# Moving silu's table load, a batch's landmark sums, w_in copies and GpSimd's load issues in a fused Nystrom attention and silu MLP kernel

## The chip, the cores and the metric

The kernel runs on one core of one Trainium2 chip. A core has five engines that each take their own list of instructions in order: TensorE (PE, matrix products; PEld is its loading of weights), VectorE (DVE), ScalarE (ACT), GpSimd (POOL) and SyncE (SP, which issues transfers). They wait for each other by semaphores. Data lie in SBUF; products arrive in PSUM, which the kernel divides into eight banks of 128 x 512 fp32. Transfers run on 16 DMA engines; most loads are issued from GpSimd's list, since they convert fp32 to bf16 on the way.

The metric is the device time of one execution in microseconds (us): 260.79 before, the median of three runs (260.73 to 262.19).

## The reference

For each of 8 batches and 8 heads, q, k and v are 576 x 64. Landmarks are means of 18 successive rows, 32 of them:

```python
q_lm = q.reshape(B, H, m, S // m, D).mean(axis=3)      # m = 32, S // m = 18
k_lm = k.reshape(B, H, m, S // m, D).mean(axis=3)
A  = sm(q, k_lm)       # softmax of scaled scores, 576 x 32
Bm = sm(q_lm, k_lm)    # 32 x 32
C  = sm(q_lm, k)       # 32 x 576
Z = Bm.transpose(0, 1, 3, 2) / (norm_1(Bm) * norm_inf(Bm) + 1e-06)
for _ in range(6):
    Z = 2 * Z - Z @ Bm @ Z
x = A @ Z @ C @ v      # heads side by side: 4608 tokens x 512
h = x @ w_in           # 512 x 2048
out = (h * sigmoid(h)) @ w_out
```

The norms are taken over each head's 32 x 32 matrix (norm_1 and norm_inf stand for numpy's matrix norms of order 1 and infinity).

## The kernel before

**The algebra.** The kernel never forms x. Per batch it makes the small matrix Z C v of each head (`zwT`, made by `z_mm` and `z_out`), multiplies it into w_in (`m_unit` or `m_pair`, result `mb`: 256 landmark rows x 2048), transposes the softmax A (`AT`), and computes h = A times mb directly: `l1_mm` (two matmuls of 128 x 128 by up to 320 columns for each of two groups of 128 hidden units, into PSUM tile `hps`), then silu on ScalarE (`l1_act`, L803, result `gT`), then the product with w_out in blocks of 128 tokens: `l2_mm` (16 matmuls of 512 columns a block into a bank `ops`, then a ScalarE copy to `ost`, L830, and a store from SyncE).

**The loop.** L936 runs over the batches b, and inside it 16 steps s (L951): steps 0 to 7 are the eight groups of hidden units for the first half of the tokens, 8 to 15 for the second. While batch b's MLP runs, the attention of batch b + 1 is worked out between its matmuls: scores and exponentials at the first steps (at s = d + 1 and d + 2, where d is 2 for b = 0 and 1 and 0 afterwards), the six iterations (`ns_mm`, `ns_step`) at the next, then `w_mm`, `x_out`, `z_mm`, and the product with w_in. The object `a` is the attention of batch b + 1, `a0` that of batch b. Batches 0 and 1 are `tiled` (products in 32 x 32 tiles, A in chunks of 128 tokens); from batch 2 on (`sub`) the scores of A are transposed by VectorE and shifted by GpSimd. The branch at L1007 (`s == d + 2 and a.sub`) runs in b = 1 to 6, once each; the branch at L1017 runs in b = 0.

**What sets the order.** The order is written out by hand: each engine takes its instructions in the order of the text, and `tc.manual_schedule()` (L77) leaves it so. `l2_mm(n)` emits the next n matmuls of a queue of blocks, and the counts `CNT` and `REST` (L841 to L844) say how many at each step, so the point at which a block of 16 ends, and its copy is emitted, follows from these counts. One `act` is ScalarE's silu; `table(func)` (L163) is a one-element activation on `spare` that makes the chip load func's table (rows L165: ACT_TABLE_LOAD, then ACTIVATE).

**PSUM.** Pools: `psh` two tiles of two banks (`hps`, scores of C `scp`, transposes `ctp` and `atp`, pairs `mpp`), `pso` two banks used in turn (`ops`, `wp`, `idle`, one half of `m_unit`'s `mp`), `psn` one bank (`bb` of the iterations, landmark sums `lmp`), `psa` one bank. A tile taken from a pool waits until all reads of the tile that held the buffer before are done.

**The head, before the loop.** q and k of batch 0 arrive, TensorE runs filler matmuls on zeros (`idle`), and the attention of batch 0 is worked out alone up to L931. The landmark sums of batch 1's first half of heads (`landmarks_pe`, 18 matmuls with the identity, L206) are put behind `z_mm` there: three ahead of the product with w_in, 15 behind the transposes of A; their ScalarE copies (`landmarks_out`, L213) come at L959.

**GpSimd.** Its list holds the issues of loads (`load_qk` L101, `load_v` L112, `load_w_in`, `load_w_out`), the multiplies of `a_norm` (L680: VectorE sum and reciprocal, then GpSimd's product `an`, L693), and, from batch 2 on, the landmark sums (`landmarks_pool`, L223: five additions, `lma` to `lmn`, for each half of the heads).

Of the kernel before, what the change touches and what calls it, by code (L numbers as in the profile page):

```python
# [9 lines left out]
BF = mybir.dt.bfloat16  # L10
# [33 lines left out]
def kernel(  # L44
# [9 lines left out]
    nc = tc.nc  # L54
# [28 lines left out]
    def ps2(nm):  # L83
        return psh.tile([128, 2, 512], FP, tag="h", name=nm)
# [832 lines left out]
    load_w_out(2)  # L917
    load_w_out(3)
    load_v(1)
    at = ps2("atp")  # L920
    a.z_mm(at[:, 1, :])
    a.z_out()
    lp = psn1("lmp")
    landmarks_pe(1, lp, 0, 2, (0, 3))

    def first_tokens():
        a.a_transpose(0, at[:, 0, :].bitcast(BF))
        a.a_out(nc.vector.tensor_copy)
        landmarks_pe(1, lp, 0, 2, (3, SEG))

    a.m_unit(0, nc.vector.tensor_copy, nc.scalar.copy, parts=2, between=first_tokens)  # L931

    ready = None
    for b in range(B):  # L936
# [14 lines left out]
        for s in range(NDC):  # L951
# [2 lines left out]
                a0.m_pair(a0.m_done)  # L954
            if s <= d and b == 0:
                l1(s)
                act(s)
                if s == 0:
                    landmarks_out(1, lp, 0, 2)  # L959
                    a0.m_unit(1, nc.scalar.copy, nc.scalar.copy)  # L960
                elif s == 1:
                    idle(lp[:, 256:512], 8, 256)
                elif s == 2:
                    landmarks_pe(1, lp, 2, 2)
                    landmarks_out(1, lp, 2, 2)
                transpose_qk(1, ORD[s])
# [5 lines left out]
            elif not nxt or s <= d:  # L972
                l1(s)
                act(s)
                n = cnt[s]
                if b == 1 and s == d:
                    a = Att(2)
                    a.lm_t(0, 2)
                if nxt and s == d and not a.early:
                    l2_mm(3)  # L980
                    n -= 3
                    a.a_pair()
                l2_mm(n)

            elif s == d + 1:
                l1(s)
                act(s)
                l2_mm(cnt[s])
                if b == 0:

                    transpose_qk(1, ORD[s])
                    a.lm_t(1)
                    a.bd_expand(0, 2, nc.gpsimd.tensor_copy)
                    for i in (1, 2):
                        a0.a_scores(i)
                        a0.a_max(i)
                a.b_scores()
                a.c_scores()
                a.b_max()
                a.c_max(0)  # L1000
                table(AF.Exp)
                if b == 0:
                    for i in (1, 2):
                        a0.a_shift(i)
                        a0.a_exp(i)
                a.b_exp()
            elif s == d + 2 and a.sub:  # L1007
                a.a_start()
                a.c_max(1)
                a.c_exp(0)  # L1010
                a.c_exp(1)
                a.a_exp_all()
                a.b_norm()
                l2_mm(cnt[s])
                table(AF.Silu)
                l1(s)
            elif s == d + 2:  # L1017
                n = cnt[s]
                a.a_start()
                a.a_scores(0)  # L1020
                a.a_scores(1)
                a.c_max(1)
                a.a_max(0)
                a.a_max(1)
                a.c_exp(0)
                a.c_exp(1)
                a.a_scores(2)
                a.a_max(2)
                for i in range(2):
                    a.a_shift(i)  # L1030
                    a.a_exp(i)
                a.b_norm()
                a.a_shift(2)
                a.a_exp(2)
                a.c_transpose(0)
                a.c_out(0)
                a0.m_unit(2, nc.vector.tensor_copy, nc.scalar.copy, pair=True)
                a.f_mm()
                a.b_scale()
                a.f_out()  # L1040
                l2_mm(n)
                table(AF.Silu)
                l1(s)
            elif b == 0:
                l1(s)
                r = s - d
                n = cnt[s]
                if r == 3:
                    nc.vector.tensor_tensor(out=parity, in0=mask[:, 0:2, 0],
                                            in1=mask[:, 2:4, 0], op=OP.add)  # L1050
                    a.ns_mm()
                    a.ns_step()
                    act(s - 1)
                    a0.m_unit(3, nc.vector.tensor_copy, nc.scalar.copy)
                    a0.a_norm(1)
                elif r == 4:
                    a.ns_mm()
                    a.c_transpose(1)
                    a.ns_step()
                    a0.a_norm(2)  # L1060
                    a.c_out(1)
                elif r == 5:
                    act(s)
                    a.ns_mm()
                    a.ns_step()
                    l2_mm(2)
                    n -= 2
                    load_v(2)
                    a.w_scale()
                    a0.a_transpose(1)  # L1070
                    a0.a_out(nc.scalar.copy)
                    a.a_norm(0)
                elif r == 6:
                    a.ns_mm()
                    a.ns_step()
                    act(s)
                    l2_mm(2)
                    n -= 2
                    a.ns_mm()
                    load_qk(3, (1, 0))  # L1080
                    a.a_norm(1)
                    a.ns_step()
                    load_qk(3, (3, 2))
                elif r == 7:
                    a.ns_mm(last=True)
                    act(s)
                    a.x_out()
                    l2_mm(2)
                    n -= 2
                    a.w_mm()  # L1090
                    a.w_out()
                    a.a_norm(2)
                    landmarks_pool(2, 0)
                elif r == 8:
                    a.z_mm(psa1("zt"))
                    a.z_out()
                    act(s)
                    l2_mm(n)
                    n = 0
                    landmarks_pool(2, 2)  # L1100
                    a.a_transpose(0)
                    a.a_out(nc.vector.tensor_copy)
                    transpose_qk(2, ORD[0])
                elif r == 10:
                    a.a_transpose(1)
                    a.a_out(nc.vector.tensor_copy)
                    transpose_qk(2, ORD[1])
                elif r > 11:
                    transpose_qk(2, ORD[r - 10])
                if s in h:  # L1110
                    act(s)
                if r in (9, 11):
                    a.m_pair(r - 9)
                l2_mm(n)
            elif s == d + 3:
                l1(s)
                act(s - 1)
                act(s)
                l2_mm(2)
                a.f_mm()  # L1120
                a.b_scale()
                a.f_out()
                a.w_scale()


                nc.gpsimd.tensor_copy(out=gate, in_=a.wsp[:, 0, :])  # L1126
                l2_mm(cnt[s] - 2)
                a.ns_mm()
            elif s <= d + 8:
                l1(s)  # L1130
                if s == d + 6:
                    a.w_mm()
                a.ns_step()
                act(s)
                if s == d + 4:
                    a.a_sum(0)
                elif s == d + 5:
                    a.a_sum(1)
                elif s == d + 6:
                    a.w_out()  # L1140
                    a.a_rec(0, 2)
                    a.a_mul(0)
                    a.a_mul(1)
                l2_mm(cnt[s])
                a.ns_mm(last=(s == d + 8))
            elif s == d + 9:
                l1(s)
                a.x_out()
                act(s)
                l2_mm(cnt[s])  # L1150
            elif s == d + 10:
                l1(s)
                a.z_mm()
                a.z_out()
                act(s)
                l2_mm(cnt[s])
            else:
                l1(s)
                act(s)
                if s in (d + 11, d + 13):  # L1160
                    a.m_pair(s - d - 11)
                n = cnt[s]
                if s == 15 and ready and ready.early:
                    l2_mm(3)
                    n -= 3
                    ready.a_pair()
                l2_mm(n)
# [62 lines left out]
```

## Time and profile before

| what | value |
|---|---|
| median of three runs | 260.79 us (260.73, 262.19, 260.79) |
| the profiled execution | 262.13 us, span 260.4 us from first to last instruction |
| busy: PE, DVE, ACT, POOL | 249.9 (96%), 166.2 (64%), 170.4 (65%), 132.8 (51%) us |
| mean granted TensorE clock | 0.991 |
| `ops` (w_out) matmuls | 592, 146.8 us busy |
| `hps` (mb) matmuls | 512, 82.9 us busy |
| silu `gT` | 128, 652 ns each |
| table loads | 16, 1283 ns each |
| `ost` copies 128 x 512 | 35 of them (and two of 128 x 256), 571 ns each |
| GpSimd's `lma` | 12, 2377 ns each |

The profile is of one execution. A line of it names the line of the program, the engine, the operation, out<-in tiles, and shapes as partitions x elements; in a timeline the first two figures are the start and the length in us from the start of the span, and a bracket at the end gives the idle time before the instruction and what ended it. Matmuls are pipelined, so the length of one (379 ns for 512 columns) is longer than the distance of two in a row (0.216 us). The granted clock is the share of TensorE's full clock; rows of 0.50 mean that its matmuls take twice as long.

### The profile page before, as it was taken

The page shows a single profiled execution, that of the slowest core. Times are in us where ns is not written, and L with a number is a line of the kernel's source. Part 1 is how long each engine was busy: PE and PEld are TensorE (multiplying, and loading weights), DVE is VectorE, ACT ScalarE, POOL GpSimd, SP SyncE. Part 2 cuts the span into 40 slices and gives each one's busy share as a digit, 9 for nine tenths or more (in the row PEclk, how much of TensorE's full clock was granted, in tenths as well). Part 3 has the DMA queues.
Part 4 walks back from the last instruction along what each step waited for, and adds up shares of the span by engine and source line. Part 5 has one row for each costly group of instructions (what it writes and reads, how often), then busy time and mean ns, then how long its engine had stood idle before and what let it go on. Part 6 is the DMA issues. An engine that isn't in the chain of part 4 may idle for free.

```text
span 260.4 us, 6656 instructions
## 1 busy us (share of the span) xinstructions
PE 249.9 (96%) x2768; PEld 139.0 (53%) x2768; DVE 166.2 (64%) x391; ACT 170.4 (65%) x311; POOL 132.8 (51%) x161
## 2 busy tenths in 40 slices
PE   8989999989899999999999999999999999999994
PEld 2646654454454556456645564545555564556553
DVE  5877876759895969777885788686977745000000
ACT  2276985677847685869575957597668857446511
POOL 7616518993699469845993298138923030100000
PEclk9997999999999999999999999999999999999998
DMA  7999999960529992895279617113621401121122
GB/s 220 195 209 207 207 208 208 224 149 5 141 24 219 228 210 49 115 192 137 55 132 205 110 45 132 42 35 111 107 66 40 120 25 42 41 80 43 42 81 82
DMA packets 30062, 31.16 MB, mean 120 GB/s; under 512 B 10960, under 2 KB 21456, under 8 KB 30032
## 3 DMA queue, kind: packets, MB, share of 16 engines
q0 software_dynamic: 14816, 17.76, 41.4%
q1 hardware_dynamic: 15216, 12.98, 16.7%
q8 instruction: 21, 0.34, 0.5%
q14 instruction: 9, 0.07, 0.1%
HBM read 36.70 MB, written 9.44 MB: 177 GB/s over the span
## 4 chain that ended last, share of the span: by engine, by line
PE 77%; ACT 6%; DVE 6%; POOL 5%; DMA 3%; issue 2%; ACTq 0%; POOLq 0%
PE ops L80 43%; PE hps L80 21%; DMA nat<-in_q_dram 3%; PE bb L80 3%; PE mp L80 2%; PE lmp L80 2%; POOL lma L229 2%; DVE cmx L448 2%; ACT L165 1%; PE sa L80 1%; ACT eC L458 1%; PE wp L80 1%; PE scp L80 1%; ACT ex L644 1%; PE mpp L80 1%
## 5 line engine op out<-in xcount | busy, mean ns | idle before, releaser
L80 PE MATMUL ops<-w_out_sb,gT 128*128 128x512 bf16 (+1 forms) x592 | 146.8, 374 | 0.0
L804 ACT ACTIVATE gT<-hps 128x576 bf16<-128x576 f32 (+2 forms) x128 | 82.6, 652 | 57.2 <-PE hps L80 56.4
L80 PE MATMUL hps<-AT,mb 128*128 128x288 bf16 (+2 forms) x512 | 82.9, 286 | 1.7 <-ACT gT L804 1.0
L80 PEld LDWEIGHTS <-gT 128*128 128x128 bf16 x592 | 53.8, 98 | 48.2 <-issue 9.0
L80 PEld LDWEIGHTS <-mb 128*128 128x128 bf16 x512 | 48.6, 98 | 28.6 <-issue 3.3
L203 DVE STREAM_TRANSPOSE qkT<-nat 128x576 f32<-128x576 f32 x32 | 39.3, 1244 | 0.3
L830 ACT COPY ost<-ops 128x512 f32<-128x512 f32 (+1 forms) x37 | 21.1, 571 | 14.3 <-PE ops L80 14.2
L229 POOL TENSOR_TENSOR lma<-nat 128x1152 f32<-128x1152 bf16 x12 | 28.5, 2377 | 0.0
L407 DVE SCALAR_TENSOR_TENSOR fx<-fx,bb 128x320 bf16<-128x320 bf16 (+1 forms) x39 | 17.0, 435 | 12.5 <-PE bb L80 12.3
L632 POOL TENSOR_TENSOR xs<-xs,nm 128x576 f32<-128x576 f32 x12 | 13.6, 1152 | 21.3 <-DVE nm L630 21.3
L770 DVE CAST mb<-mp 128x512 bf16<-128x512 f32 x28 | 18.0, 684 | 7.4 <-PE mp L80 7.4
L165 ACT ACT_TABLE_LOAD x16 | 20.5, 1283 | 1.1 <-PEq L1214 0.8
L688 POOL TENSOR_TENSOR an<-ex,arec 128x576 bf16<-128x576 bf16 x12 | 13.6, 1158 | 5.3 <-DVE arec L674 5.3
L1126 POOL COPY gate<-wsp 128x2 f32<-128x2 f32 x6 | 1.1, 184 | 28.6 <-DVE wsp L492 28.6
L80 PEld LDWEIGHTS <-fx 32*32 32x32 bf16 (+1 forms) x168 | 8.2, 93 | 12.3 <-DVE fx L407 4.4
L771 ACT CAST mb<-mpp 128x1024 bf16<-128x1024 f32 x14 | 14.2, 1012 | 0.1
L80 PE MATMUL bb<-fx 32*32 32x64 bf16 (+2 forms) x168 | 13.1, 205 | 0.6 <-DVE fx L407 0.3
L626 DVE STREAM_TRANSPOSE xs<-sa 128x576 f32<-128x576 f32 x12 | 8.7, 762 | 6.9 <-PE sa L80 6.9
L234 POOL TENSOR_TENSOR lmc<-lmb,lma 128x384 f32<-128x384 f32 x12 | 12.0, 998 | 0.9
L232 POOL TENSOR_TENSOR lmb<-lma 128x384 f32<-128x384 f32 x12 | 12.0, 996 | 0.9
L448 DVE TENSOR_REDUCE cmx<-scp 128x1 f32<-128x576 f32 x16 | 11.9, 751 | 0.5 <-PE scp L80 0.3
L659 DVE TENSOR_REDUCE arec<-ex 128x18 f32<-128x576 bf16 (+2 forms) x17 | 11.8, 694 | 0.0
(126 smaller groups left out, 263.8 us busy)
## 6 DMA issues: line engine op xcount, KB each, us to landing
out_dram<-ost SPq DMA_DIRECT2D x35, 256.0 KB, 2.0
v<-in_v_dram POOLq DMA_DIRECT2D x8, 576.0 KB, 6.8
nat<-in_k_dram POOLq DMA_DIRECT2D x15, 288.0 KB, 9.3
nat<-in_q_dram POOLq DMA_DIRECT2D x15, 288.0 KB, 10.1
w_in_sb<-in_moe_w_in_dram POOLq DMA_DIRECT2D x4, 512.0 KB, 15.2
w_out_sb<-in_moe_w_out_dram POOLq DMA_DIRECT2D x4, 512.0 KB, 14.1
raw<-in_k_dram SPq DMA_DIRECT2D x1, 576.0 KB, 4.1
raw<-in_q_dram SPq DMA_DIRECT2D x1, 576.0 KB, 5.0
```

The lines of the kernel that those rows point to most:

```text
L80: nc.tensor.matmul(out=o, lhsT=lhsT, rhs=rhs, start=start, stop=stop, skip_group_check=True)
L165: nc.scalar.activation(out=spare[:, 1:2], in_=spare[:, 0:1], func=func)
L203: nc.vector.transpose(out=o.rearrange("p (l t) -> p t l", t=SEG), in_=nat_t[b][:, j, :].bitcast(FP).rearrange("p (t l) -> p t l", l=L))
L229: nc.gpsimd.tensor_tensor(out=a1, in0=nat[:, :, 0:3 * w], in1=nat[:, :, 3 * w:6 * w], op=OP.add)
L407: nc.vector.scalar_tensor_tensor(out=n, in0=self.fx, scalar=2.0, in1=self.p, op0=OP.mult, op1=OP.add if self.tiled else OP.subtract)
L448: nc.vector.tensor_reduce(out=mx, in_=self.s[g][:, :, 0:HF], op=OP.max, axis=AX.XY, negate=True)
L632: nc.gpsimd.tensor_tensor(out=self.xs[:, i], in0=self.xs[:, i], in1=self.nm[:, i].unsqueeze(3).to_broadcast((128, 2, SEG // 2, L)), op=OP.add)
L688: nc.gpsimd.tensor_tensor(out=self.an[:, i].rearrange("p r t l -> p (r t) l"), in0=x, in1=r.unsqueeze(2).to_broadcast((128, SEG, L)), op=O ...
L770: nc.vector.tensor_copy(out=o[:, r, 0:512], in_=m[r])
L771: nc.scalar.copy(out=o[:, :, 512:1024], in_=m2)
L804: nc.scalar.activation(out=gT_t[b][:, 2 * s:2 * s + 2, o + c0:o + c1], in_=h[:, :, 0:c1 - c0], func=AF.Silu)
L830: nc.scalar.copy(out=ost[:, 0:hi - lo], in_=st["ps"][:, 0:hi - lo])
```

## The change

Six edits, all of them in the order of the text; no computation is added or taken away but three filler matmuls.

- The landmark sums of batch 1's first half of heads go to a bank of `pso` in place of `psn`; ten of the 18 matmuls stand ahead of `z_mm`, eight behind `z_out`, and their two copies on ScalarE follow at once. The tile `lmp` in `psn` is then taken at step 0 of the loop.
- The transposes of A and their copy come ahead of the product with w_in, whose `between` goes away.
- The second unit of the w_in product moves from step 0 to step 1, with its copies in halves and `act(1)` between them; five fillers stand at step 1 in place of eight.
- In the branch of batches 2 on (L1007), `table(AF.Silu)` stands directly behind the exponentials, ahead of `b_norm` and `l2_mm`, in place of behind `l2_mm`. In the branch of batch 1 (L1017) it stands behind the last `a_exp`, ahead of the third w_in unit and all that follows.
- That third unit comes ahead of `c_transpose(0)` and `c_out(0)`, and both of its copies are VectorE's.
- GpSimd's issues of v of batch 2 and q and k of batch 3 are spread over steps r = 3 to 6: v and the first ahead of `a0.a_norm(1)`, the others one at a time behind `a0.a_norm(2)`, `a.a_norm(0)` and `a.a_norm(1)`, where there were two pairs around `a.a_norm(1)`.

```diff
     load_v(1)
+    lp = pso1("lmp")
+    landmarks_pe(1, lp, 0, 2, (0, 10))
     at = ps2("atp")
     a.z_mm(at[:, 1, :])
     a.z_out()
-    lp = psn1("lmp")
-    landmarks_pe(1, lp, 0, 2, (0, 3))
-
-    def first_tokens():
-        a.a_transpose(0, at[:, 0, :].bitcast(BF))
-        a.a_out(nc.vector.tensor_copy)
-        landmarks_pe(1, lp, 0, 2, (3, SEG))
-
-    a.m_unit(0, nc.vector.tensor_copy, nc.scalar.copy, parts=2, between=first_tokens)
+    landmarks_pe(1, lp, 0, 2, (10, SEG))
+    landmarks_out(1, lp, 0, 2)
+    a.a_transpose(0, at[:, 0, :].bitcast(BF))
+    a.a_out(nc.vector.tensor_copy)
+    a.m_unit(0, nc.vector.tensor_copy, nc.scalar.copy, parts=2)
...
                 l1(s)
-                act(s)
                 if s == 0:
-                    landmarks_out(1, lp, 0, 2)
-                    a0.m_unit(1, nc.scalar.copy, nc.scalar.copy)
+                    act(s)
+                    lp = psn1("lmp")
                 elif s == 1:
-                    idle(lp[:, 256:512], 8, 256)
+                    a0.m_unit(1, nc.scalar.copy, nc.scalar.copy, parts=2,
+                              between=lambda: act(1))
+                    idle(lp[:, 256:512], 5, 256)
                 elif s == 2:
+                    act(s)
                     landmarks_pe(1, lp, 2, 2)
...
                 a.a_exp_all()
+
+                table(AF.Silu)
                 a.b_norm()
                 l2_mm(cnt[s])
-                table(AF.Silu)
                 l1(s)
...
                 a.a_exp(2)
+                table(AF.Silu)
+                a0.m_unit(2, nc.vector.tensor_copy, nc.vector.tensor_copy, pair=True)
                 a.c_transpose(0)
                 a.c_out(0)
-                a0.m_unit(2, nc.vector.tensor_copy, nc.scalar.copy, pair=True)
                 a.f_mm()
                 a.b_scale()
                 a.f_out()
                 l2_mm(n)
-                table(AF.Silu)
                 l1(s)
...
                     a0.m_unit(3, nc.vector.tensor_copy, nc.scalar.copy)
+                    load_v(2)
+                    load_qk(3, (1,))
                     a0.a_norm(1)
...
                     a0.a_norm(2)
+                    load_qk(3, (0,))
...
-                    load_v(2)
...
                     a.a_norm(0)
+                    load_qk(3, (3,))
...
-                    load_qk(3, (1, 0))
                     a.a_norm(1)
+                    load_qk(3, (2,))
                     a.ns_step()
-                    load_qk(3, (3, 2))
```

## The prediction

> **What bounds the kernel now.** I read the page's chain first, then the chain in order of time, then the granted clock by windows, and last the queues around each moved line.
>
> The page's shares of the chain that ended last:
>
> ```profile
> PE 77%; ACT 6%; DVE 6%; POOL 5%; DMA 3%; issue 2%; ACTq 0%; POOLq 0%
> ```
>
> TensorE carries it, so an edit counts only if it moves TensorE's queue or one of the few pieces that are not PE. The chain in order of time, from 45 us (start, length, what):
>
> ```profile
> 45.92 0.63 POOL an L693
> 46.56 2.33 POOL lma L229
> ...
> 57.70 0.32 DVE lmc L271
> 58.07 0.50 PE sa L80 x16
> ...
> 66.10 1.28 ACT L165
> 67.60 0.55 ACT gT L804
> 68.19 0.65 PE hps L80 x4
> ```
>
> From 43.8 to 68.2 the chain runs over GpSimd's landmark sums of batch 2, their scores and maxima on VectorE, the exponentials and silu's table; TensorE idles 0.84 us at 58.07 and 0.95 us at 68.19 and is continuously busy after that. So whatever happens before 46 us counts only as far as it moves the first `lma` (L229).
>
> Third, the clock windows (stretch, length, PE busy, ..., PEclk as the third figure from the end):
>
> ```profile
> 16.65:20.06 3.41, 2.69 (x95) 1.59 (x94) 2.09 (x10) 2.71 (x5) 0.97 (x2) 1.00 1.20 208
> 20.06:23.48 3.42, 3.17 (x31) 2.48 (x31) 2.31 (x6) 1.61 (x5) 3.42 (x6) 0.50 1.15 207
> ```
>
> The profiled execution (262.13 us: span 260.4 and 1.73 around it) had half a clock from 20.06 to 23.48 us, where the batch 1 landmark sums (15 matmuls, 1.81 us; 18 take 1.17 at full clock) held up the first `l1` until 23.28. At full clock these 15 take 15 x 0.057 = 0.86 from about 21.1 and end at 21.97, when the three ScalarE copies of w_in's product (1.07 from 20.95) are nearly done too: 1.31 earlier. The profiled time is 1.34 over the median of 260.79, so I take the median run to be one without that window.
>
> **The head, edits one by one.** The landmark sums: 18 before and after, ten now beside the wait for `x_out` (TensorE idle 19.33 to 19.76, ten take 10 x 0.057 = 0.57, so `z_mm` comes up to 0.1 later) and eight beside `z_out`; their two copies (0.34) go to ScalarE where it is free after its table (20.65). A^T (4 matmuls 0.61, copy 0.43) ahead of the w_in product (8 matmuls 0.41): 0.3 later for the product, but the first `l1` no longer waits for landmark sums: about 21.7. The second w_in unit split around `act(1)` and five idles for eight (1.03/8 = 0.13 each) let `l1(2)` start before all four copies are done: about 0.15. All this is at most 0.5 us against the median run, 1.3 against the profiled one. Around 33 us silu's table moves ahead of a w_in copy that now goes to VectorE: ScalarE's wait (0.45) and copy (0.59) leave its queue, VectorE gets 0.68 more ahead of `c_out` and `b_scale`, so `f_out` ends 0.7 later, 0.1 behind the point at which TensorE asks for it (35.95). Net 0 to 0.2 lost there.
>
> What does it bring at `lma`? Two clocks stand before it. One is GpSimd's queue: four `nat` issues (1.14 and 1.13 us) stood between `an` 42.6 and 45.92; two of them are moved, worth up to 1.1. The other is the load. A landing time (the last figure, us from issue) and a wait that shows how GpSimd's issues are paced:
>
> ```profile
> nat<-in_q_dram POOLq DMA_DIRECT2D x1, 288.0 KB, 15.2
> POOL nat L108 <- DMA w_out_sb<-in_moe_w_out_dram: 1.0, 1, 1.0
> ```
>
> The first is batch 2's q half, issued 29.86: lands 45.06, behind a queue that has moved 207 GB/s without a pause since 5 us. `lma` reads it, so it can't start before about 45.36 (0.3 is what the other wait shows from landing 31.66 to issue 31.94): 1.15 before the profiled 46.5, and no earlier whatever GpSimd does. The wait says that the 20th issue waited for the 12th to land (the 10th and 11th waited for the 2nd and 3rd). So in the new places batch 3's first half, the 22nd, waits for the third w_out load (21.78 + 15.0 = 36.8), ahead of `a0.a_norm(1)`: its multiply starts at about 37.6 (38.34 before; about 37.0 in the median run). The 24th waits for v (23.26 + 18.9 = 42.2), the 25th for batch 2's first half (29.31 + 14.3 = 43.6); `a_norm(2)` ends near 45.2. GpSimd is thus paced by landings, and `lma` comes at 45.36 with or without the slow clock. In the median run GpSimd's old order gives 42.4, 43.45, 44.8, 45.45: the same landing. So the head gains 1.15 against the profiled execution and 0 against the median (bounds: 0.4 gained, 0.6 lost if `a_transpose(1)`, now at 39.3 behind that multiply, costs more than TensorE's slack at 58.07). Take 0. GpSimd's issues with v and batch 3 cost no one else: same order, and their data is used after 68 us.
>
> **The table in the sub-batch branch.** This is the edit with a price. In L1007-1016, run once each in b = 1 to 6, the load moves from behind `l2_mm` to ahead of it. `l2_mm` emits, when a block of 16 matmuls is full, the copy `ost` (L830) that frees its PSUM bank; that copy is now queued on ScalarE behind the table load (1.28) and silu's first use (0.20). ScalarE in b = 3 now (start, length, what):
>
> ```profile
> 117.55 1.15 ACT L639 ACTIVATE ex<-xs 128x1152 bf16<-128x1152 f32 x1
> 118.60 0.57 ACT L830 COPY ost<-ops 128x512 f32<-128x512 f32 x1
> 119.19 1.28 ACT L165 ACT_TABLE_LOAD   x1
> 120.48 0.20 ACT L165 ACTIVATE spare<-spare 128x1 f32<-128x1 f32 x1
> 120.59 1.17 ACT L804 ACTIVATE gT<-hps 128x576 bf16<-128x576 f32 x2
> ```
>
> The copy follows the exponential without a gap, so the load gains nothing by passing it: silu still starts at 120.59. The copy ends at about 120.69 (exponential to 118.70, load to 120.00, first use, copy from 120.12), not 119.17. Who waits? The pool `pso` has two banks, so the first matmul of the block after next. TensorE in that stretch, and the `ops` matmuls started before 119.57:
>
> ```profile
> 118.94 2.32 PE L80 MATMUL ops<-w_out_sb,gT 128*128 128x512 bf16 x10
> L80 PE MATMUL ops<-w_out_sb,gT x192: 379/379/390, 34.1 to 119.4; 128*128 128x512 bf16 x192
> ```
>
> 192 is 12 x 16: the next block's first matmul is the fourth of those ten, 118.94 + 3 x 0.216 = 119.59. It needs the bank whose copy ends at 120.69; with 0.06 to wake (silu's end 177.54 to `hps` 177.60) it starts at 120.75: **1.16 us lost**. The same count for the others. b = 2: 128 matmuls started before 93.43, so the ninth block begins at 93.43; exponential to 91.90, copy to 93.89, wake 93.95: **0.52**. b = 5: 336 before 175.69; exponential to 175.02, copy to 177.01, start 177.07 against 175.70: 1.37, of which 0.20 was already lost (`hps` at 177.60 waits for silu, 0.39 behind the matmul before it instead of 0.19): **1.17**. b = 4 and 6 end their second block one matmul into the next step (149.79 against a copy to 148.49), and in b = 1 the block after next begins after 72 us: 0. Sum **2.85 us**, with nothing behind it to give it back: TensorE is busy 30.00 of 30 us from 100 to 160.
>
> Sum on the profiled execution: 262.13 - 1.15 + 2.85 = 263.83; on the median, 260.79 + 0 + 2.85 = 263.64. I say 263.7, 1.1% over the median; about 1% (2.6 us) is what a measurement of this kernel tells from no change.
>
> **What the Trainium skill says.** TensorE: Matmul & The Clock Gate, section "Why this matters for your kernels", has the clock drop only after gaps of about 3 us; by that rule my stalls of 0.5 to 1.2 us cost themselves alone and the sum stays. The row above speaks against it: the longest gap from 16.65 to 20.06 was 0.43 us, and the clock fell.
>
> **Rivals.**
> 1. The copies come in time (the other side). A bank is late only if the 1.5 us by which the copy moves exceed its margin now: 93.43 - 92.38 = 1.05, 119.59 - 119.17 = 0.42, 175.70 - 175.49 = 0.21. If the exponentials end 1.3 us earlier against TensorE, nothing is lost, and the head decides: 260.4 to 261.3, not slower. Against: the scores and maxima ahead of them are where they were. 0.07 (0.01 of it below 258.2).
> 2. Part is given back: `lma` sits on GpSimd's issues in the median run too, so the head gains up to 1.1, or later waits such as the 0.2 in b = 5 absorb it: 261.6 to 262.8. The landing of 45.06 speaks against. 0.13.
> 3. The head loses: `a0.a_norm(1)` behind a later landing, past the slack at 58.07: 264.4 to 265.2. 0.06.
> 4. A stall starves a clock window: 3.41 us at half clock lose 1.7 us each, 265.3 for one, 268.7 for three. The 0.95 us gap at 67.2 to 68.2 among dense matmuls left the clock at 1.00, which speaks against. 0.06.
> 5. A load behind a long exponential first empties the engine for as long as a load lasts: three stalls by 1.3 more, 267.5. 0.02.
> The Trainium skill, ScalarE: Activation LUTs, section "What ACT_TABLE_LOAD costs", states such a drain, 1.38 us beside a load of 1.28; by it the three stalls would be 7.0 us and the time 267.8. The rows differ: the ten loads after 86 us start 0.02 behind the instruction before them (114.00 behind a silu that ended at 113.98).
>
> The forecast holds 0.66, by itself 263.1 to 264.4 (`lma` between 0.6 and 1.3 earlier than profiled; the stall in b = 2 between 0 and its 0.5), 0.46 of it above the 263.4 that is 1%. Slower 0.46 + 0.06 + 0.06 + 0.02 = 0.60, within 0.39, faster 0.01. The range reaches over rival 2 and half of rival 3: 261.6 to 264.9.
>
> **What will show it.** ScalarE's list with the load directly behind `ex` and `ost` behind it in b = 2, 3, 5; `ops` waiting for `ost` there, about 0.5, 1.2, 1.4; the same places in b = 4 and 6 without a wait; `lma` at 45.2 to 45.6; the first `l1` near 22. Wrong if `ops` shows no wait for L830, or if `lma` starts well before 45.

## The result, and the profile after

The changed kernel takes 263.47 us (median of 8 runs, 262.97 to 263.54). The kernel before, run beside it, has a median of 261.53 (8 runs, 260.69 to 262.34). The ratio is 1.0071, with a 95% interval of 1.0048 to 1.0094: slower, by less than 1%.

To read this ratio one must know that executions of the kernel before come in two kinds. Some have a granted clock of 0.997 or more and take 260.4 to 261.2 us; the others have 0.991 to 0.993 and take 261.9 to 262.4, which is the window at half a clock that the prediction found in the profiled execution. Over all comparisons of this study 45 of 117 executions before were of the second kind (one more, a disturbed one of 266.4 us, is left out). The changed kernel had none in 8. So the change costs 2.8 us against the first kind, 1.2 against the second, and 0.7% against the mixture. Below, "full clock" and "half clock" name the two kinds; before they have medians of 260.71 and 262.29.

The profiled execution after is 263.16 us (span 261.4). Its shares of the chain that ended last:

```profile
PE 70%; ACT 9%; DVE 9%; POOL 5%; issue 3%; DMA 2%; ACTq 0%; POOLq 0%
```

ScalarE has 9% where it had 6. The 3% of issue are not to be read as time: this profile lists 554 `ops` matmuls in place of 592, and where a record is missing, the trace shows a short idle time without a cause. The other waits of TensorE (what waits, line, for whom; us in total, times, longest):

```profile
PE ops L80 <- issue: 4.1, 26, 0.2
PE ops L80 <- ACT ost L830: 2.5, 3, 1.2
PE idle L80 <- DVE zero L130: 1.3, 1, 1.3
PE hps L80 <- ACT gT L804: 1.0, 1, 1.0
```

The second line is new. Three times the w_out matmuls wait for `ost`, ScalarE's copy out of a PSUM bank. One of them in the timeline, b = 3 (start, length, what; in brackets the idle time before it and who ended it):

```profile
116.28 1.15 ACT L639 ACTIVATE ex<-xs 128x1152 bf16<-128x1152 f32 x1
...
117.44 1.28 ACT L165 ACT_TABLE_LOAD   x1
...
118.74 0.20 ACT L165 ACTIVATE spare<-spare 128x1 f32<-128x1 f32 x1
118.85 0.57 ACT L830 COPY ost<-ops 128x512 f32<-128x512 f32 x1
...
119.31 1.19 ACT L804 ACTIVATE gT<-hps 128x576 bf16<-128x576 f32 x2
...
119.47 1.67 PE L80 MATMUL ops<-w_out_sb,gT 128*128 128x512 bf16 x7 [0.99 <-ACT ost L830]
```

The load stands directly behind the exponential, the copy behind the load, and the seven matmuls start 0.05 behind the copy's end at 119.42. The three matmuls ahead of them started at 117.67, so without the wait the next would have come at 117.67 + 3 x 0.216 = 118.32: 1.15 us are lost. The other two places:

```profile
92.21 1.02 PE L80 MATMUL ops<-w_out_sb,gT 128*128 128x512 bf16 x4 [0.35 <-ACT ost L830]
...
176.92 1.46 PE L80 MATMUL ops<-w_out_sb,gT 128*128 128x512 bf16 x6 [1.20 <-ACT ost L830]
```

Worked out in the same way from the rows ahead of them, they lose 0.51 (92.21 against 90.40 + 6 x 0.216) and 1.36 (176.92 against 174.91 + 3 x 0.216). The brackets are smaller than the losses, since they count from the modelled end of the matmul before.

The first half of the chain, in order of time:

```profile
43.59 0.40 POOL nat L108
43.98 0.17 issue
44.16 0.63 POOL an L693
44.78 2.33 POOL lma L229
...
55.94 0.32 DVE lmc L271
56.30 0.50 PE sa L80 x14
...
62.80 1.05 ACT ex L639
63.87 1.28 ACT L165
65.19 0.09 issue
65.27 0.57 ACT ost L830
65.84 0.56 ACT gT L804
66.44 0.65 PE hps L80 x4
```

`lma` starts 1.77 us before its place in the profile of before (46.50), which is of the half-clock kind. In the kernel's old order at full clock it starts at 45.00 (traces of experiments 2 and 3), so against that it gains 0.27. In b = 1 the copy `ost` stands between table and silu, where it delays no bank. The clock (stretch, length, then for each engine busy time and instructions, PEclk third from the end):

```profile
16.84:20.25 3.41, 2.61 (x104) 2.02 (x98) 2.20 (x10) 2.96 (x5) 1.25 (x3) 1.00 1.20 209
20.25:23.67 3.42, 2.87 (x39) 1.70 (x37) 2.94 (x6) 2.55 (x10) 3.42 (x5) 1.00 1.18 208
```

Where the profile of before had 0.50 there is 1.00.

### The profile page after: what moved, and what is told of

Read it like the earlier page. It is cut to its first block, busy times and chain, and to the rows that moved or that the text cites. A ratio compares the mean times of both kernels' runs of the same rounds, so it can differ in the third digit from the quotient of the medians.

```text
span 261.4 us, 6609 instructions
## 1 busy us (share of the span) xinstructions
PE 242.5 (93%) x2723; PEld 137.0 (52%) x2765; DVE 166.2 (64%) x392; ACT 170.5 (65%) x312; POOL 133.1 (51%) x161
## 4 chain that ended last, share of the span: by engine, by line
PE 70%; ACT 9%; DVE 9%; POOL 5%; issue 3%; DMA 2%; ACTq 0%; POOLq 0%
PE ops L80 38%; PE hps L80 20%; PE bb L80 3%; DVE cmx L448 3%; ACT L165 2%; PE lmp L80 2%; PE mp L80 2%; POOL lma L229 2%; ACT ex L639 2%; DMA raw<-in_k_dram 2%; ACT eC L458 1%; PE sa L80 1%; POOL an L693 1%; PE wp L80 1%; ACT ost L830 1%
## 5 line engine op out<-in xcount | busy, mean ns | idle before, releaser
L80 PE MATMUL ops<-w_out_sb,gT 128*128 128x512 bf16 (+1 forms) x554 | 139.7, 373 | 7.0 <-issue 4.1
```

The source lines that it names most:

```text
L80: nc.tensor.matmul(out=o, lhsT=lhsT, rhs=rhs, start=start, stop=stop, skip_group_check=True)
```

## The experiments

For each kernel the medians at full and at half clock are given, with the number of runs, and the ratio with its interval to all runs of the kernel before on the same chip.

**1. The table edit taken back.** After, but for the branch of batches 2 on.

```diff
-                table(AF.Silu)
                 a.b_norm()
                 l2_mm(cnt[s])
+                table(AF.Silu)
```

> The changed kernel with one edit undone: in the branch of batches 2 on, silu's table stands behind l2_mm again. Theory S (the table edit in b = 2, 3 and 5 is the whole loss, 0.51 + 1.15 + 1.36 us in the changed kernel's trace): 263.47 - 2.8 = 260.6 to 260.8, with no wait of ops for ost, and all runs close together (260.4 to 261.0), since the changed kernel showed no execution with a half clock in the head. Theory H (the head's edits or GpSimd's issues carry a part of the loss): 261.5 or more in runs at full clock.

Measured: 260.72 in all 12 runs' median (260.53 to 261.02), none at half clock; 0.9983 [0.9965, 1.0002]. No `ops` matmul waits for a copy. The one edit is worth 263.47 - 260.72 = 2.75 us, and all others together 0.0 at full clock.

**2. The table edit alone**, the same two lines the other way round in the kernel before.

> The kernel before with that edit alone. Theory S: 2.7 us on top of either group of before's runs, so 263.4 at full clock (before 260.7) and 264.9 where the head has its half clock (before 262.2); waits of ops for ost of about 0.5, 1.15 and 1.35 us. Theory H: under 262.5 in the faster runs.

Measured: 263.44 (4 runs) and 265.05 (2 runs); 1.0106 [1.0073, 1.0140]. The waits of TensorE show the same line as after:

```profile
PE ops L80 <- ACT ost L830: 2.5, 3, 1.2
```

Its price is 2.73 at full clock and 2.76 at half clock: it adds to the window of the head and does not depend on it.

**3. The early table only where no bank should be late**, in b = 1, 4 and 6 of the kernel before.

```diff
                 a.a_exp_all()
+                if b in (1, 4, 6):
+                    table(AF.Silu)
                 a.b_norm()
                 l2_mm(cnt[s])
-                table(AF.Silu)
+                if b not in (1, 4, 6):
+                    table(AF.Silu)
```

> The kernel before with the table ahead of l2_mm only in b = 1, 4 and 6, where the block after next begins after its bank's copy. Theory S (a bank that comes late, not the order itself, is the price): no change, 260.7 and 262.2 by group, no wait of ops for ost. Rival O (each early load costs something of its own, by an order on ScalarE that is worse everywhere): half of the six moves, about 1.4 us slower.

Measured: 260.85 (8 runs) and 262.24 (4 runs); 1.0005 [0.9982, 1.0027]. The largest waits of TensorE, in which `ops` is absent:

```profile
PE idle L80 <- DVE zero L130: 1.3, 1, 1.3
PE lmp L80 <- DVE qkT L203: 1.2, 1, 1.2
PE hps L80 <- ACT gT L804: 1.0, 1, 1.0
```

The order itself costs nothing to be seen (0.1). The price sits in b = 2, 3 and 5, the steps that the count of blocks had named.

**4. The table stays early, the copies go to VectorE** (after, in that branch only), so that nothing is queued behind the load.

```diff
-    def l2_mm(n):
+    def l2_mm(n, copy=nc.scalar.copy):
...
-                nc.scalar.copy(out=ost[:, 0:hi - lo], in_=st["ps"][:, 0:hi - lo])
+                copy(out=ost[:, 0:hi - lo], in_=st["ps"][:, 0:hi - lo])
...
-                l2_mm(cnt[s])
+                l2_mm(cnt[s], nc.vector.tensor_copy)
```

> The changed kernel with the ost copies that fall into the step of the early table load given to VectorE. Theory S: TensorE waits for the copy, not for ScalarE as such, so the three waits of ops for ost vanish and the time is at most that of the kernel with the table put back, 260.7; moreover in b = 1 silu starts a copy (0.5 us) earlier and TensorE's wait for it there (1.0 us) shrinks by that: 260.2. Rival V (VectorE, which has scores, b_scale and the transposes to do at that time, hands the delay on): 261 or more.

Measured: 260.55 (12 runs, 260.11 to 261.02, none at half clock); 0.9963 [0.9943, 0.9983]. The copy in b = 1, and what is left of the wait for silu:

```profile
63.04 0.68 DVE L830 COPY ost<-ops 128x512 f32<-128x512 f32 x1
...
64.18 1.28 ACT L165 ACT_TABLE_LOAD   x1
```

```profile
PE hps L80 <- ACT gT L804: 0.5, 1, 0.5
```

The three waits are gone with the table still early, so it is the copy in ScalarE's queue and not the load that TensorE waited for. The wait for silu falls from 1.0 to 0.5, but the kernel is only 0.17 faster than with the table taken back. Where the other 0.3 goes was not found.

**5. The head's edits alone** (landmark sums, A^T, w_in's second unit) on the kernel before.

> The kernel before with the head's edits alone (landmark sums around z, A^T ahead of w_in, second w_in unit around act(1), five fillers). If the ten sums in the wait for x_out keep the clock up: no run with a half clock between 18 and 24 us, all runs 260.5 to 261.0. If the half clock has another cause (where the executions fall against the clock's windows): two groups about 1 us or more apart as before. First l1 at about 21.8 in a run at full clock, and the first lma (L229) no more than 0.4 us earlier than at full clock before, since a landing paces it.

Measured: 260.50 (12 runs, 260.17 to 260.67, none at half clock); 0.9972 [0.9954, 0.9991]. At full clock they gain 0.2. In the trace the first `l1` starts at 21.82 and `lma` at 44.75, 0.25 before its 45.00 in the old order. What they do beside that is to make the half clock go away. All kernels of this study that have these edits, the changed one among them, show no run at half clock in 92; four that have the old head (experiments 2, 3, 6 and 7) show 14 in 42.

**6. GpSimd's issues alone** on the kernel before.

> The kernel before with GpSimd's issues alone moved. Theory L (the first lma is paced by landings in either order: the 24th issue waits for v, the q half of batch 2 lands at 44.4 to 45.0): no change at full clock, 260.6 to 260.9, lma at 44.9 to 45.1; and with the half clock in the head less of a loss, since GpSimd's queue no longer carries it on: the slower group falls from 262.2 to about 261.2. Rival G (GpSimd's own issues set lma): up to 1.1 faster in both groups.

Measured: 260.82 (6 runs) and 261.73 (6 runs); 0.9996 [0.9975, 1.0018]. At full clock nothing, as expected. At half clock 0.56 less than before, about half of what was expected: the window costs 0.9 in place of 1.58. In its profiled execution (half clock) `lma` starts at 46.13, only 0.37 before its place in the profile of before. The new places are not enough to make GpSimd's late start good. The place that was expected at full clock, 44.9 to 45.1, is not tested: this is the only trace.

**7. The table and w_in copies around 33 us alone.**

```diff
                 a.a_exp(2)
+                table(AF.Silu)
+                a0.m_unit(2, nc.vector.tensor_copy, nc.vector.tensor_copy, pair=True)
                 a.c_transpose(0)
                 a.c_out(0)
-                a0.m_unit(2, nc.vector.tensor_copy, nc.scalar.copy, pair=True)
...
                 l2_mm(n)
-                table(AF.Silu)
```

> The kernel before with the edits of the branch of batch 1 alone (silu's table behind the last a_exp, third w_in unit ahead of c_transpose and copied by VectorE). By the prediction 0 to 0.2 us lost there and nothing at the end, since lma does not move: 260.7 to 260.9 at full clock, two groups as before.

Measured: 260.67 (10 runs) and 261.92 and 262.23 (2 runs); 0.9976 [0.9954, 0.9998]. No loss.

**8. Which part of the head keeps the clock: the ten sums in the gap?** After with the table taken back, and all 18 landmark sums behind `z_out`, none beside the wait for `x_out`.

```diff
     lp = pso1("lmp")
-    landmarks_pe(1, lp, 0, 2, (0, 10))
     at = ps2("atp")
     a.z_mm(at[:, 1, :])
     a.z_out()
-    landmarks_pe(1, lp, 0, 2, (10, SEG))
+    landmarks_pe(1, lp, 0, 2, (0, SEG))
```

> The changed kernel with the table put back and with all 18 landmark sums behind z_out, none in the wait for x_out. Theory C (the ten sums in that wait keep the clock up): executions with a half clock from about 20 us come back, as a part of the runs 0.3 us or more above the rest, less than the 1.4 of before because lma is paced by landings. Rival: the clock holds without them, and all runs stay within 260.5 to 261.1.

Measured: 260.78 (12 runs, 260.47 to 261.15, none at half clock); 0.9973 [0.9953, 0.9994]. The clock holds without the ten matmuls in the gap, so that theory falls.

**9. Or the bank?** The kernel before, with nothing changed but the pool of the landmark sums, which then need not wait until `z_out` has read the bank.

```diff
     a.z_out()
-    lp = psn1("lmp")
+    lp = pso1("lmp")
     landmarks_pe(1, lp, 0, 2, (0, 3))
...
                     landmarks_out(1, lp, 0, 2)
+                    lp = psn1("lmp")
```

> The kernel before with the landmark sums' bank alone changed (pso for psn), so that the three sums behind z_mm need not wait for z_out (0.3 us) and nothing else moves. If that idle stretch is what lets the clock fall: no slower group, all runs near 260.7. If it is the sum of the head's rearrangement (A^T, no 15 sums in front of the first l1): two groups as before, 260.7 and 262.2, about a third of the runs in the slower.

Measured: 260.57 (12 runs, 260.29 to 260.91, none at half clock, while 9 of 28 runs of the kernel before on that chip were); 0.9974 [0.9954, 0.9994]. The first three sums in the timeline of before, and of this kernel:

```profile
20.31 0.48 PE L80 MATMUL lmp<-nat,ident 128*128 128x128 bf16 x3 [0.31 <-DVE zwT L541]
```

```profile
19.78 0.34 PE L80 MATMUL lmp<-nat,ident 128*128 128x128 bf16 x3
```

The wait of 0.31 is gone, and no run is at half clock. At the share of the kernel before (45 of 117) none in 12 would come by chance once in some 300 times, at 9 of 28 once in 100, so the change of bank very probably removes it. How is not shown, and the wait itself can hardly be the cause: in the profile of before it lasts from 20.00 to 20.31, and the clock had fallen at 20.06.

**10. Head and early table with VectorE's copies**: experiments 4 and 5 together, with GpSimd's issues and the stretch around 33 us as before.

> The kernel before with the head's edits, silu's table ahead of l2_mm and the ost copies of that step on VectorE; GpSimd's issues and the branch of batch 1 as before. The head's edits alone gave 260.50; the copy on VectorE took TensorE's wait for silu in b = 1 from 1.0 to 0.5 us, so 260.2 (0.3 to 0.5 less) with no slower group. If VectorE hands delays on, 260.5 or more.

Measured: 260.37 (12 runs, 260.09 to 260.74, none at half clock); 0.9966 [0.9947, 0.9985]. Of the early table's 0.5 in b = 1 only 0.13 shows against experiment 5.

**11. Is `lma` held by GpSimd's issues or by the landing?** Experiment 10 with all four loads of batch 3 behind the landmark sums.

```diff
-                    load_qk(3, (1, 0))
                     a.a_norm(1)
                     a.ns_step()
-                    load_qk(3, (3, 2))
...
                     landmarks_pool(2, 2)
+                    load_qk(3)
```

> The same with the four loads of batch 3 issued behind the landmark sums of batch 2 instead of between the three a_norm. Theory L: GpSimd is then free for lma once the q half of batch 2 has landed (44.4 to 45.0 in the runs so far) and a_norm(2) is done (about 43.9), so lma comes at 44.4 to 44.8, at most 0.4 earlier: 259.9 to 260.2. Rival G (the issues were what held it): lma at 43.9 and 0.9 us gained.

Measured: 261.40 (12 runs, 260.83 to 262.01); 1.0010 [0.9990, 1.0030], 1.0 over experiment 10. With the issues out of the way `lma` waits for the load, 0.27 before its place in experiment 10:

```profile
44.37 2.37 POOL L229 TENSOR_TENSOR lma<-nat 128x1152 f32<-128x1152 bf16 x1 [0.23 <-DMA nat<-in_q_dram]
```

The gain is lost 15 us later. VectorE scales a column of maxima, `bbs`, in experiment 10 and here:

```profile
59.62 0.44 DVE L304 TENSOR_SCALAR bbs<-bmx 128x2 f32<-128x2 f32 x1
```

```profile
59.35 1.71 DVE L304 TENSOR_SCALAR bbs<-bmx 128x2 f32<-128x2 f32 x1
```

and TensorE then waits for the exponentials of C, 1.1 us at once:

```profile
PE hps L80 <- ACT eC L458: 1.5, 3, 1.1
```

**12. Only the second pair of issues moved**, to the step of b = 1 behind `a_pair`, past the stretch that experiment 11 disturbed.

```diff
                     a.a_norm(1)
                     a.ns_step()
-                    load_qk(3, (3, 2))
...
                     a.a_pair()
+                    if b == 1:
+                        load_qk(3, (3, 2))
```

> The kernel with the head's edits and the ost copies on VectorE, with only the second pair of batch 3's loads moved, to behind GpSimd's two additions of b = 1 (L632, ended at 61.1 us). Theory L: lma comes with the landing, 44.1 to 44.4, 0.3 earlier, and since GpSimd's two additions again wait for VectorE one by one, the scaling bbs (L304) takes 0.44 and not the 1.71 us that it took where all four loads had been put behind the landmark sums: 260.0 to 260.2. If that 1.71 came from the later loads themselves and not from how GpSimd's and VectorE's instructions met, it is there again: 261 or more.

Measured: 260.02 (12 runs, 259.56 to 260.33, none at half clock); 0.9946 [0.9926, 0.9967]. `bbs` takes 0.44 again, and `lma` again waits for the load:

```profile
45.10 2.37 POOL L229 TENSOR_TENSOR lma<-nat 128x1152 f32<-128x1152 bf16 x1 [0.81 <-DMA nat<-in_q_dram]
```

This is the fastest kernel of the study, 0.5% under the one before (0.7 us, or 0.3%, under its runs at full clock) and 1.3% under the changed one (3.45 us). But `lma` was expected at 44.1 to 44.4, and here it is later than in experiment 10 (44.64). The profiled execution is the kernel's slowest (260.33), with a late landing; in the others the load may land earlier, but no trace shows it, so where the 0.35 over experiment 10 comes from stays open.

## Why the prediction was right or wrong

**The table edit: right in place, cause and size.** The prediction had 0.52, 1.16 and 1.37 us for b = 2, 3 and 5 and nothing for 1, 4 and 6. The trace has 0.51, 1.15 and 1.36, in these three places only; experiment 3 shows the other three to be free, experiments 1 and 2 the edit to be the whole loss, experiment 4 the queued copy to be its cause. The sum was 2.85; the trace gives 3.02, less the 0.20 that b = 5 lost before, 2.82; the times give 2.75 and 2.73. What made it come out was to count blocks of 16 from the number of matmuls started, so that the matmul which needs the late bank was known by its place and its start. Rival 1 (the copies come in time) and rival 2 (part given back) are out.

**The other edits at full clock: right.** 0 was forecast with bounds of 0.4 gained and 0.6 lost; experiment 1 measures 0.0. The single pieces lie between 0.2 gained (head) and 0.1 lost (GpSimd), and around 33 us the loss of up to 0.2 did not come, so rival 3 is out. The first `l1` starts at 21.80 (21.7 forecast), only 0.07 before its place in the old order at full clock (21.87, experiments 2 and 3).

**The landing as the bound of `lma`: the mechanism right, the size off.** The rows of GpSimd in the profile after:

```profile
36.68 0.54 POOL L108 DMA_DIRECT2D nat<-in_k_dram  x1 [1.73 <-DVE fx L407]
37.29 1.62 POOL L693 TENSOR_TENSOR an<-ex,arec 128x512 bf16<-128x512 bf16 x2
...
41.87 0.59 POOL L108 DMA_DIRECT2D nat<-in_k_dram  x1 [1.06 <-DMA v<-in_v_dram]
...
44.73 2.37 POOL L229 TENSOR_TENSOR lma<-nat 128x1152 f32<-128x1152 bf16 x1
```

The 24th issue waits for v, as was worked out, and the multiply comes at 37.29 (37.6 forecast). But `lma` started at 44.73, outside the 45.2 to 45.6 that were forecast. Two terms of "no earlier than 45.36" were too large: the load lands at 44.4 after (issued 28.11, 16.3 us), not 45.06, and the 0.3 taken for the wake-up is 0.08 in experiment 12 (issued 28.12, 16.9 us, start 45.10) and 0.17 in experiment 11 (28.10, 16.1, 44.37). So at full clock landing and issues end nearly together: `lma` waits for neither alone in the changed kernel, and for the landing once the issues are moved (experiments 11 and 12).

The prediction put the old order at full clock at the same 45.36 and had no trace of it. Experiment 3 has one:

```profile
45.00 2.37 POOL L229 TENSOR_TENSOR lma<-nat 128x1152 f32<-128x1152 bf16 x1
```

Both places were thus forecast late by about as much (0.36 and 0.63), and their difference, which is what counts, came out at 0.27, and at 0.09 in experiment 1 (`lma` at 44.91), where 0 was forecast. The sum held because both places were off the same way. Rival 2 had up to 1.1 here, and no gain reached the end in experiment 1.

**The half clock: the window was read rightly, its place in the sum was not.** The step that failed is "I take the median run to be one without that window". The 260.79 shown was such a run, but more than a third of the executions are not, so the kernel before measures 261.53 beside the changed one. The absolute time was then close (263.7 said, 263.47 measured, within 263.1 to 264.4), while the difference was 1.9 instead of 2.85 and fell under 1%, where 0.60 had been put on more. The step also let GpSimd's pacing by landings make the slow clock indifferent. Experiment 6 shows that the new issues bring back 0.56 of 1.58. What takes the window away is the new head (0 of 92 runs) and very probably already its change of bank (experiment 9), which the prediction counted only for its place in the queue. That the changed kernel would have no run at half clock was nowhere argued; as far as its median rests on that, the close absolute time is luck.

**The stalls and the clock.** Rival 4 (a stall starves a window) did not come: stalls of 0.5 to 1.4 us left the clock at 0.997 or more in all 8 runs. With that the rule of the Trainium skill, TensorE: Matmul & The Clock Gate, section "Why this matters for your kernels", agrees, which asks for no gap over about 3 us if the clock is to stay up. The head speaks against it: in the profile of before the clock fell at 20.06 behind gaps of at most 0.43 us.

**The drain.** Rival 5 did not come either. The Trainium skill, ScalarE: Activation LUTs, section "What ACT_TABLE_LOAD costs", has 1.38 us of draining beside a load of 1.28; here the exponential ended at 117.43, the load started at 117.44 and took 1.28.

## What to carry to other kernels

Before a long instruction is moved forward in an engine's queue, list what is thereby queued behind it, and for each of these find the buffer it frees and the instruction that takes that buffer next: with two banks, the first matmul of the block after next, whose start can be counted out of the trace (here the three losses came out to within 0.01 us). If the queued work is a copy out of PSUM, give it to another engine before moving the load. And look at the spread of the times shown: three runs with one 1.4 us off may be two kinds of execution, and a change that removes one of them shifts the median without touching the other.

## What was not expected of the hardware

**Whether the half clock comes seems to hang on where the clock's windows begin, and on the order of the head.** The kernel before has it in 45 of 117 executions, 1.58 us each. In its profile the clock fell at 20.06 and once more behind the last matmuls, at 258.99; in that of experiment 6 at 20.54 and 259.47. Both pairs lie 238.93 us apart, which is 70 times 3.413, about the length of the half clock. So the fall at the end, which every trace has, is taken here to tell where the windows of that execution begin. The rows of experiment 6 (fell), and of experiment 8 (held), whose clock fell last at 259.19, 70 windows behind 20.26:

```profile
17.12:20.53 3.41, 2.44 (x86) 1.00 1.19 210
20.53:23.94 3.41, 3.41 (x33) 0.50 1.18 208
...
16.84:20.25 3.41, 2.76 (x99) 1.00 1.21 208
20.25:23.67 3.42, 2.88 (x43) 1.00 1.16 208
```

There are five profiles with the old head. A window ends at 20.06 (before) and 20.54 (experiment 6), where the clock fell, and at 19.52 (experiment 7), 21.05 (experiment 3) and 21.82 (experiment 2), where it held. A stretch of 1.3 us in 3.41 would give the 45 of 117. With the new order of experiment 8 a window ends at 20.26, between the two, and the clock held: so the place of the windows alone doesn't decide. The profiles of the changed kernel (18.69) and of experiment 9 (18.99) have no end of a window there and can't tell. What the clock counts stays open: TensorE's work in the window, of which some records may be missing, is 2.69 and 2.44 us where it fell, and 2.60 (17.63 to 21.05, experiment 3) and 2.76 (experiment 8) where it held.

**A VectorE instruction on two columns took 1.71 us.** In experiment 11 `bbs` ran from 59.35 to 61.06, and GpSimd's two additions ran back to back:

```profile
58.72 2.30 POOL L632 TENSOR_TENSOR xs<-xs,nm 128x576 f32<-128x576 f32 x2
```

They end at 61.02, so `bbs` ended with the second. In experiment 10 the additions run from 58.87, the first to 60.03 and the second to 61.14, and `bbs` ends at 60.06, with the first. In all 14 profiles `bbs` takes 0.43 or more, where its neighbour `cbs`, as small, takes 0.15. It looks as if `bbs` waits for GpSimd's running instruction. Not every VectorE instruction does: in experiment 11 `bmx`, just ahead of it, ran from 59.10 to 59.31 beside the first addition. The wait agrees with the Trainium skill, Trainium Architecture — The Big Picture, section "What this means for kernel authors", by which the port pair that VectorE and GpSimd share is an exclusive lock. Why VectorE got in between the two additions in one case and not in the other is open; in both they follow each other without a gap.
